# Attention and two MoE layers in one kernel: a new load order, and a new order of the prologue and the ramp

## The chip, the cores and the metric

The kernel runs on one core of a Trainium2 chip. The metric is the time of one execution on the device, in microseconds (us); lower is better. Five engines work side by side, each on its own queue of instructions in a fixed order, and wait for one another by semaphores: PE (TensorE, matrix products), DVE (VectorE), ACT (ScalarE), POOL (GpSimd) and SP (SyncE, which here only issues transfers). Transfers (DMA) are issued from SP's queue and a few from ACT's.

## What is computed

The reference is an attention with pooled keys, and two gated layers behind it:

```python
kv_pool = kv.reshape(B, H // 4, 4, W // 4, 4, C).mean(axis=(2, 4))
k = v = kv_pool.reshape(B, -1, C) @ w_sr            # 768 keys, C = 128
s = (q @ k.T) / sqrt(C)
a = exp(s - s.max(-1)); a /= a.sum(-1) + 1e-9
x = a @ v                                           # 12288 rows of 128
h = x @ moe_w_in;   x = (h * clip(h + 3, 0, 6) / 6) @ moe_w_out     # d_ff = 2048
h = x @ moe2_w_in;  g = where(h >= 1, h, where(h <= -1, 0, (h + 1)**2 / 4))
out = g @ moe2_w_out
```

The weights of the two layers reach the kernel as 64-bit floats, two 32-bit words for an element.

## The kernel before, in words

The 12288 rows are cut into 24 blocks of 512. A block needs its scores (four tiles of 128 rows by 768 keys, `s_mm`), a softmax (`s_max`, `s_exp`, `s_sum`, `a_hi`, `a_lo`), a transpose of the result by DMA, the product with v (`av`), and then layer 1 and layer 2. A layer's 2048 inner columns are walked in eight steps of two slices of 128, and such a step is one *slot*: layer 2 runs 11 slots (`O2`) behind layer 1, and the scores of the next block run beside both. 192 steps of layer 1 follow each other this way. From slot 16 on the order of a slot's parts is the list `SLOT`; the first slots have lists of their own, `RAMP0` and then `RAMP`, and the last ones `TAIL`. All order is written out by hand in these strings, letter by letter; no scheduler moves anything within an engine.

Numbers are kept as pairs of fp16 tiles, a high and a low part, and a product takes three fp16 matmuls (`m_in`, line 759; `m_out`, line 784). Some steps of `m_out` are listed as *whole* (`F32A` for layer 1, `F32` for layer 2): there the fp32 tile itself goes into one fp32 matmul, and the cast (`cast`, line 860) and the low part (`low`, line 868) are left out. `CAST_P` lists the casts that run on POOL instead of ACT, `A_P` the softmax tiles whose fp16 parts are made on POOL (lines 674 and 687) instead of ACT and DVE (676 and 689), `HALF_T` those whose high and low part are transposed by a DMA each (681 and 694) instead of one together (696), `ALT` a second way to make layer 2's activation.

Ahead of the first slot is the prologue, the string `PROLOGUE`: each word is a step, and after each step `load_next` issues as many further loads as there are free buffers. `LOADS` is the order of the loads: `k5` is tile 5 of kv (12 tiles), `w` the next piece of a weight (16 pieces: the four input pieces of layer 1, its four output pieces, then the same of layer 2), `q0` the rows of block 0. All tiles of kv and of the weights are 512 KB and share 17 buffers (12 of tag `wst`, 3 of `g2`, 2 of `t1`); a kv tile frees its buffer when it is pooled, a weight piece when it is converted. k0, k2 and q0 are issued from ACT's queue, all others from SP's (`kv_load`, `q_load`, `w_load`, lines 358, 572, 209 and 212).

The steps of the prologue that matter here:

- `mN`: the largest absolute value of weight piece N, a reduction on DVE (`w_max`, line 229). Even N below 8 are layer 1's input pieces, odd ones its output pieces; 8 to 15 the same of layer 2. `ia it ib ic` make layer 1's input scale from the four maxima by way of PE, `oa ot ob oc` its output scale; `a2 b2 s2` and `a3 b3 s3` do so for layer 2.
- `jN.0`, `jN.1`, `jN.2`: the three stages of converting piece N: two operations on ACT (lines 300 and 302), two on DVE (314 and 316), a cast and a low part on POOL (337 and 340).
- `kN`: pooling of kv tile N on PE. `KV_MODE` has a letter for each tile: P pools with the pooling matrix as the weight (line 387) and needs a copy on ACT and a transpose for each pair of tiles; D takes the tile as the weight (line 392); G adds on POOL first, and a `gN` step does two matmuls (line 407).
- `tM pM zM yM`: keys and values of a group of 128 keys, `q0` and `q1` the transposed and split rows of a block, `vm vr vs vh vl` the scale and the two parts of v.
- `sJ SJ nJ NJ eJ aJ bJ`: block 0's softmax for its tile J: scores of the first and of the second half of the keys, their maxima on DVE, the exponential on ACT, the reciprocal and the high part, the low part with its transpose.
- `x0`, `x1`: the product with v for the two halves of the block, with its high part on ACT and its low part on DVE. After them the first slot begins with `m_in`.
- `d`: an idle matmul on PE whose result is not used.

`MX` hangs prologue steps on slots: in the kernel before it holds seven of layer 2's eight maxima (slots 0 to 3) besides the scales. `CONV_AT` lists the slots in which the remaining nine pieces begin their conversion, `EARLY` the slots of the scores and products of blocks 1 and 2, `SPLIT_AT` those whose scores are done in two halves in the banks of `h` instead of the one score bank.

The loop that plays a slot's list:

```python
def slot(T):
    for n, g in orders[(T >= R0_T) + (T >= RAMP_T) + (T >= TAIL_T)]:
        at, f = ops[n]
        for t in range(served.get(n, 0), T - g + 1):
            key = at(t)
            if key is not None:
                f(*key)
        served[n] = max(served.get(n, 0), T - g + 1)
```

## Time and profile before

| | us |
|---|---|
| median of 3 runs | 1265.27 (1265.13 to 1265.32) |
| the profiled execution | 1266.3 |
| its span, first to last instruction | 1264.5 |
| PE busy in the span | 1230.8 |
| DVE, ACT, POOL busy | 1121.5, 1100.2, 1042.0 |

The span is the part of an execution that the trace covers; 1.8 us of the execution lie around it. A matmul's end is modelled, so a busy PE is not PE at its peak. In the rows further down, "idle before <- releaser" is the time an engine stood still before an instruction, and whose result it had waited for.

### The profile page before, as it was taken

The page shows a single profiled execution, that of the slowest core. Times are in us where ns is not written, and L with a number is a line of the kernel's source. Part 1 is how long each engine was busy: PE and PEld are TensorE (multiplying, and loading weights), DVE is VectorE, ACT ScalarE, POOL GpSimd, SP SyncE. Part 2 cuts the span into 40 slices and gives each one's busy share as a digit, 9 for nine tenths or more (in the row PEclk, how much of TensorE's full clock was granted, in tenths as well). Part 3 has the DMA queues.
Part 4 walks back from the last instruction along what each step waited for, and adds up shares of the span by engine and source line. Part 5 has one row for each costly group of instructions (what it writes and reads, how often), then busy time and mean ns, then how long its engine had stood idle before and what let it go on. Part 6 is the DMA issues. An engine that isn't in the chain of part 4 may idle for free.

```text
span 1264.5 us, 18732 instructions
## 1 busy us (share of the span) xinstructions
PE 1230.8 (97%) x6259; PEld 654.7 (52%) x6259; DVE 1121.5 (89%) x1861; ACT 1100.2 (87%) x1918; POOL 1042.0 (82%) x959
## 2 busy tenths in 40 slices
...
DMA packets 260945, 66.30 MB, mean 52 GB/s; under 512 B 252528, under 2 KB 256752, under 8 KB 260848
## 3 DMA queue, kind: packets, MB, share of 16 engines
...
## 4 chain that ended last, share of the span: by engine, by line
PE 92%; DVE 4%; DMA 2%; ACT 1%; issue 0%; SPq 0%; DVEq 0%; ACTq 0%
PE acc L784 39%; PE h L759 37%; PE s L613 7%; PE s L708 7%; DMA wst<-in_kv_dram 1%; PE s L759 1%; DMA wst<-in_moe_w_out_dram 1%; PE h L387 1%; PE h L708 0%; DVE t L818 0%; DVE g L833 0%; DMA wsr<-in_w_sr_dram 0%; DVE g L849 0%; DVE wst L316 0%; DVE acc L314 0%
## 5 line engine op out<-in xcount | busy, mean ns | idle before, releaser
L868 POOL TENSOR_TENSOR l<-g,h 128x512 f16<-128x512 f32 x351 | 402.8, 1166 | 84.7 <-DVE a L689 57.9
L868 POOL TENSOR_TENSOR l<-t,h 128x512 f16<-128x512 f32 x365 | 431.2, 1202 | 6.5 <-ACT h L860 6.3
L833 DVE TENSOR_SCALAR g<-h,bs 128x512 f32<-128x512 f32 x360 | 274.0, 800 | 31.7 <-PE h L759 31.5
L811 ACT ACTIVATE t<-h,h_sc 128x512 f32<-128x512 f32 x384 | 254.1, 676 | 30.6 <-PE h L759 25.6
L849 DVE SCALAR_TENSOR_TENSOR g<-g,bs,h 128x512 f32<-128x512 f32 x374 | 263.8, 741 | 15.8 <-ACT g L844 13.1
L844 ACT ACTIVATE g<-g,bs 128x512 f32<-128x512 f32 x360 | 243.7, 716 | 18.0 <-DVE g L833 17.4
L818 DVE SCALAR_TENSOR_TENSOR t<-t,h 128x512 f32<-128x512 f32 x384 | 252.8, 679 | 6.0 <-ACT t L811 2.2
L860 ACT CAST h<-g 128x512 f16<-128x512 f32 x346 | 198.3, 614 | 46.9 <-PE acc L784 46.0
L860 ACT CAST h<-t 128x512 f16<-128x512 f32 x361 | 208.2, 616 | 4.9 <-DVE t L818 3.9
L759 PE MATMUL h<-xh,wi0h 128*128 128x512 f16 x384 | 146.4, 381 | 1.4 <-DVE t L818 1.0
L759 PE MATMUL h<-xl,wi0h 128*128 128x512 f16 x384 | 145.5, 379 | 0.1
L759 PE MATMUL h<-xh,wi0l 128*128 128x512 f16 x384 | 145.5, 379 | 0.0
L759 PE MATMUL h<-x2l,wi1h 128*128 128x512 f16 x374 | 141.7, 379 | 0.9 <-POOL x2l L545 0.9
L759 PE MATMUL h<-x2h,wi1l 128*128 128x512 f16 x374 | 141.7, 379 | 0.0
L759 PE MATMUL h<-x2h,wi1h 128*128 128x512 f16 x374 | 141.7, 379 | 0.0
L784 PE MATMUL acc<-l,wo0h 128*128 128x512 f16 x365 | 138.3, 379 | 0.7 <-POOL l L868 0.7
L784 PE MATMUL acc<-h,wo0h 128*128 128x512 f16 x365 | 138.3, 379 | 0.4 <-DVE bs L519 0.4
L784 PE MATMUL acc<-h,wo0l 128*128 128x512 f16 x365 | 138.3, 379 | 0.0
L784 PE MATMUL acc<-h,wo1h 128*128 128x512 f16 x354 | 134.2, 379 | 0.0
L784 PE MATMUL acc<-h,wo1l 128*128 128x512 f16 x354 | 134.2, 379 | 0.0
L784 PE MATMUL acc<-l,wo1h 128*128 128x512 f16 x354 | 134.2, 379 | 0.0
L759 PEld LDWEIGHTS <-wi1h 128*128 128x128 f16 x768 | 75.0, 98 | 94.0 <-issue 5.5
...
## 6 DMA issues: line engine op xcount, KB each, us to landing
out_dram<-o SPq DMA_DIRECT2D x94, 64.0 KB, 1.9
q<-in_q_dram SPq DMA_DIRECT2D x92, 64.0 KB, 2.3
wst<-in_kv_dram SPq DMA_DIRECT2D x7, 512.0 KB, 8.9
wst<-in_moe_w_out_dram SPq DMA_DIRECT2D x7, 512.0 KB, 6.2
wst<-in_moe_w_in_dram SPq DMA_DIRECT2D x6, 512.0 KB, 9.7
...
t<-in_kv_dram SPq DMA_DIRECT2D x3, 512.0 KB, 8.3
g<-in_moe_w_in_dram SPq DMA_DIRECT2D x2, 512.0 KB, 5.2
```

The lines of the kernel that those rows point to most:

```text
L387: nc.tensor.matmul(ps[p0:p0 + 32, :128], pool_m, t[:, g, j], start=(j == 0), stop=(j == 3))
L613: nc.tensor.matmul(ps[h], l[:, js], r[:, ks], start=(n == 0), stop=(n == 2))
L708: nc.tensor.matmul(ps, l[:, k, :], r[:, k, :], start=(n == 0), stop=(n == 3 * KC - 1))
L759: nc.tensor.matmul(ps, l[:, ws], r, start=(n == 0), stop=(n == 2))
L784: nc.tensor.matmul(acc[m], l[:, ws], r[:, k, :], start=(c == 0 and i == 0), stop=(c == NPAIR - 1 and i == len(order) - 1))
L811: nc.scalar.activation(out=g_t[0, s][:, k], in_=h_t[0, s, k], func=ACTF.Relu, scale=h_sc, bias=0.5 * H_SC)
L818: nc.vector.scalar_tensor_tensor(out=g, in0=g, scalar=H_SC, in1=h_t.pop((0, s, k)), op0=ALU.min, op1=ALU.mult)
L833: nc.vector.tensor_scalar(out=g_t[1, s][:, k], in0=h_t[1, s, k], scalar1=bs_t[s // NPAIR][:, 6:7], scalar2=bs_t[s // NPAIR][:, 7:8], op0=A ...
L844: nc.scalar.activation(out=g, in_=g, func=ACTF.Square, scale=bs_t[s // NPAIR][:, 8:9], bias=0.5)
L849: nc.vector.scalar_tensor_tensor(out=g, in0=g, scalar=bs_t[s // NPAIR][:, 6:7], in1=h_t.pop((1, s, k)), op0=ALU.mult, op1=ALU.max)
L860: (nc.gpsimd.tensor_copy if pool else nc.scalar.copy)(out=hl_t[m, s][0][:, k], in_=g_t[m, s][:, k])
L868: eng.tensor_tensor(out=lo[:, k], in0=g_t[m, s][:, k], in1=hi[:, k], op=ALU.subtract)
```

## The change

Only the tables of the order change; no function does. The loads begin with layer 1's weights. All eight maxima of layer 2 become steps of the prologue, in the later part of block 0's softmax and around `x0` and `x1`, and only the scales stay in `MX`. The conversions of pieces 1, 3 and 5 of layer 1 begin earlier in the prologue, and `j2.2` moves into it. Kv tiles 2 and 3 instead of 0 are pooled by mode D, and no tile by mode G. `RAMP0` serves two slots instead of four, and `RAMP0` and `RAMP` have a new order. The lists that choose engines and forms in the first slots change in some entries: `F32A` goes from 19 entries to 16 (slots 0 to 3 lose one each), `F32` from 30 to 32, `ALT` from 20 to 19, `A_P` from 7 to 9, `SPLIT_AT` from 1 to 4.

```diff
-LOADS = "k0 w w k5 k1 k6 w k4 w k3 k2 w k7 q0 k11 k8 w k10 k9 w w w w w w q2 q1 w w w w"
-KV_MODE = "DGPPPPPPPPPP"
+LOADS = "w w k0 w w w k3 w k2 k1 k5 k4 w w k7 k6 k8 k9 q0 k10 k11 w w w w q2 w q1 w w w"
+KV_MODE = "PPDDPPPPPPPP"
 PROLOGUE = """
-m0 k5 m2 g5 k4 k6 k3 m6 m4 ia it ib k1 k2 ic j4.0 t1 j2.0 g4 t2 k0 p1 j4.1 g3 g1 g9 j0.0 g2 k7 j2.1
-j4.2 t3 p3 y1 z1 t0 p0 g8 q0 m3 z0 p2 z3 k8 k11 g10 z2 j0.1 j6.0 j6.1 j6.2 g6 m1 m5 y0 m7 k10 k9 t5
-s0 t4 p5 p4 z5 s1 z4 oa S0 n1 j0.2 s2 y4 S2 n0 S1 N0 n2 N2 N1 d ot y3 e0 y2 e2 e1 a0 y5 s3 vm S3 a1
-a2 d g0 b0 n3 vr b1 vs vh d d d N3 d ob d d e3 b2 g7 q1 d oc a3 vl j5.0 b3 d hs g11 j3.0 j5.1 j3.1 d
-m9 j1.0 x0 Y x1 j1.1 j5.2 j1.2 d j3.2
+m2 m6 m0 m4 ia it m1 ib k3 k0 ic j0.0 j0.1 j2.0 k1 m3 j2.1 t0 j2.2 m5 j4.0 k2 j4.1 m7 t1 k4 oa j0.2
+p0 p1 z0 k5 z1 t2 y0 ot ob j6.0 oc j6.1 j1.0 k7 k6 t3 j4.2 k8 p3 j3.0 k9 y1 p2 k10 j1.1 q0 z2 j3.1 t4
+k11 s0 z3 t5 p4 y2 y3 p5 z4 y4 z5 S0 s2 s1 n0 n1 j5.0 S1 N0 S2 d j5.1 N1 e0 e1 s3 a0 n2 n3 y5 d N2 vm
+m12 vr d e2 b0 S3 a2 a1 N3 d vs e3 b2 q1 a3 vh b1 vl m14 j6.2 b3 m8 m15 d d hs m9 x0 m11 j1.2 m13 Y
+x1 m10 j5.2 d d d j3.2
 """
...
-R0_T = 4
+R0_T = 2
...
-a0 A0 C0:1 G:2 A1 y:1 e:1 o:2 a1 x T:3 f L1:1 B1:2 C1:1 D:1 K0 s Y K1 L0:1 v r0 Q0 O:2 t:1 R:1 r1 H:2
-Q1 l1:1 m0 u:1 c0 U:3 P:1 l0:1 z X0 i:1 F:1 B0:1 j:1 m1 B2:3 X1 n c1 w:1 q
+F:2 G:2 a0 o:2 u:2 A0 H:2 B1:2 a1 O:2 z:1 Y e:1 y:1 x T:4 X1:1 L0:1 r0 C0:1 D:1 K0 t:1 i:1 C1:1 q f
+U:4 A1 m0 v R:1 s w:2 l1:1 L1:1 r1 m1 j:1 B2:4 Q0 K1 B0:1 P:1 c0 X0 c1 l0 n Q1
...
-A_P = ((0, 2), (1, 0), (1, 1), (1, 2), (1, 3), (2, 1), (2, 3))
-HALF_T = ((0, 0), (0, 3), (1, 0), (1, 1), (1, 3))
+A_P = ((0, 0), (0, 2), (1, 0), (1, 1), (1, 2), (2, 0), (2, 2), (2, 3), (3, 0))
+HALF_T = ((0, 1), (0, 2), (0, 3), (1, 1), (1, 3))
...
-F32A = ((0, 0), (0, 1), (1, 0), (1, 1), (2, 0), (2, 1), (3, 0), (3, 1), (4, 0), (5, 0), (5, 1), (6, 0), (7, 0), (8, 1), (9, 0), (10, 0), (10, 1), (11, 0), (12, 1))
+F32A = ((0, 1), (1, 1), (2, 1), (3, 1), (4, 0), (5, 0), (6, 0), (7, 0), (7, 1), (9, 0), (9, 1), (10, 0), (10, 1), (11, 0), (11, 1), (12, 0))
...
-MX = ((0, 'j2.2 m8'), (1, 'm12 m15 m13'), (2, 'm10'), (3, 'm14 a2 m11'), (4, 'b2'), (5, 's2 a3 b3'), (6, 's3'), (7, 'bk'))
+MX = ((2, 'a2 b2'), (3, 'a3 s2'), (4, 'b3'), (5, 's3'), (7, 'bk'))
...
-CONV_AT = (2, 4, 5, 7, 8, 9, 10, 11, 12)
-EARLY = (0, 1, 2, 3, 5, 6, 4, 5, 8, 9, 10, 13, 0)
+CONV_AT = (2, 3, 4, 7, 8, 9, 10, 11, 12)
+EARLY = (0, 1, 2, 3, 5, 6, 4, 5, 8, 10, 9, 13, 0)
...
-SPLIT_AT = (6,)
+SPLIT_AT = (0, 6, 7, 9)
```

## Rows read from the trace of the kernel before

**Rows 1.** The page's first part: busy us, share of the span, instructions.

```profile
PE 1230.8 (97%) x6259; PEld 654.7 (52%) x6259; DVE 1121.5 (89%) x1861; ACT 1100.2 (87%) x1918; POOL 1042.0 (82%) x959
```

**Rows 2.** Timeline of PE, first `m_in`: start, duration, line, out<-in, [idle before <-releaser].

```profile
53.92 0.38 PE L759 MATMUL h<-xh,wi0h 128*128 128x512 f16 x1 [0.35 <-ACT xh L716]
```

**Rows 3.** Sum of the stretches from 53.92 to 120 us: length, busy us by engine.

```profile
sum 66.08, PE 60.52 PEld 33.98 DVE 60.20 ACT 48.43 POOL 50.66; mean PE 4.66 PEld 2.61 DVE 4.63 ACT 3.73 POOL 3.90
```

**Rows 4.** Stretches of ten us: busy us (instructions), PE clock, DMA share, GB/s.

```profile
20.00:30.00 10.00, 8.54 (x98) 7.35 (x96) 7.09 (x23) 6.54 (x18) 3.24 (x3) 1.00 1.08 377
30.00:40.00 10.00, 7.32 (x82) 5.93 (x74) 9.80 (x27) 5.53 (x17) 4.20 (x5) 1.00 0.84 274
```

**Rows 5.** Waits of PE from 53.9 to 120 us: total, times, longest.

```profile
PE acc L784 <- DVE su L662: 1.5, 1, 1.5
PE h L759 <- DVE t L818: 1.0, 2, 0.8
...
PE s L613 <- ACT e L653: 0.8, 1, 0.8
PE acc L784 <- POOL l L868: 0.7, 1, 0.7
```

**Rows 6.** Timeline of DVE: maxima of weights, first conversion step, softmax maxima, low part.

```profile
17.12 1.28 DVE L229 TENSOR_REDUCE mw<-wst 128x1 f32<-128x512 f32 x2 [9.11 <-DMA wst<-in_moe_w_in_dram]
...
23.69 0.69 DVE L314 SCALAR_TENSOR_TENSOR wa<-wa,wr 128x512 uint32<-128x512 uint32 x1 [0.71 <-ACT wr L302]
...
33.17 1.27 DVE L229 TENSOR_REDUCE mw<-wst 128x1 f32<-128x512 f32 x2
...
36.93 0.16 DVE L622 TENSOR_TENSOR nm<-n 128x1 f32<-128x1 f32 x1
...
48.21 1.03 DVE L689 SCALAR_TENSOR_TENSOR a<-e,rc,a 128x768 f16<-128x768 f32 x1
...
60.55 1.28 DVE L229 TENSOR_REDUCE mw<-wst 128x1 f32<-128x512 f32 x2 [1.00 <-DMA wst<-in_moe_w_out_dram]
```

**Rows 7.** DMA issues by line: size, us from issue to landing (k9; q0's first piece).

```profile
t<-in_kv_dram SPq DMA_DIRECT2D x1, 512.0 KB, 8.8
...
q<-in_q_dram ACTq DMA_DIRECT2D x1, 64.0 KB, 7.8
```

**Rows 8.** Timeline of ACT: its first instruction, a copy, a conversion's two operations, an exponential.

```profile
18.01 1.28 ACT L397 ACT_TABLE_LOAD   x1 [18.01 <-DMA q<-in_q_dram]
19.30 0.27 ACT L397 COPY e<-h 128x128 f32<-128x128 f32 x1
...
22.33 0.77 ACT L300 ACTIVATE wa<-wst,ws 128x512 f32<-128x512 f32 x1
22.99 0.67 ACT L302 ACTIVATE wr<-wst 128x512 int32<-128x512 uint8 x1
...
37.13 0.58 ACT L647 ACTIVATE e<-h,nm 128x384 f32<-128x384 f32 x1 [3.22 <-DVE nm L622]
```

**Rows 9.** Timeline of SP's queue: the issue of k9.

```profile
21.55 0.37 SPq L358 DMA_DIRECT2D t<-in_kv_dram  x1
```

**Rows 10.** Timeline of POOL: low part of a softmax tile, of a slot's step, a cast.

```profile
44.19 1.64 POOL L687 TENSOR_TENSOR a<-e,a 128x768 f16<-128x768 f32 x1
...
79.61 1.15 POOL L868 TENSOR_TENSOR l<-t,h 128x512 f16<-128x512 f32 x1
...
94.00 0.61 POOL L860 CAST h<-t 128x512 f16<-128x512 f32 x1 [2.00 <-DVE t L818]
```

**Rows 11.** Chain that ended last: start, us, four fp32 and six fp16 products.

```profile
65.99 1.72 PE acc L784 x4
67.71 1.29 PE h L759 x6
```

**Rows 12.** Waits of SP's queue up to 80 us: total, times, longest.

```profile
SPq L209 <- DMA g<-in_kv_dram: 3.0, 1, 3.0
```

**Rows 13.** Stretches of two us, columns as in rows 4.

```profile
40.00:42.00 2.00, 1.52 (x5) 1.33 (x6) 1.60 (x7) 2.00 (x5) 0.00 (x0) 0.54 0.82 119
```

More of the change, by code (lines that the diff above doesn't have):

```diff
@@ L35 @@
 W_DT = (FP16, FP16)
-R0_T = 4
+R0_T = 2
 RAMP_T = 16
 RAMP0 = """
-G:1 a0 H:4 a1 i:1 v:1 Y:1 c0 l1:2 Q1:1 F:2 e:1 s x A0:2 f X1 r0 K1:1 Q0:1 B2:3 B0:1 c1 K0:1 C1:3 R:3
-m1:1 t:1 D:2 j:3 L0:3 U:4 n B1:2 q m0 u:2 A1 P:3 y:1 l0 w:2 L1:2 o:1 X0 z T:4 C0 r1 O:2
+Q0 x Q1:1 F:3 U:3 a0 o:2 f:1 C1:2 z:1 K1:1 s l1:1 r0 B1:3 K0:2 a1 L1:3 G:2 R:2 A1 T:4 m0 B0:2 X0:2
+q:1 e:1 r1 Y:1 w:2 D:1 t:1 c0 C0 y v n P:1 j:2 B2:1 X1:2 l0 i:1 O:2 u:1 m1 L0:3 H:4 A0:2 c1
 """
 RAMP = """
-a0 A0 C0:1 G:2 A1 y:1 e:1 o:2 a1 x T:3 f L1:1 B1:2 C1:1 D:1 K0 s Y K1 L0:1 v r0 Q0 O:2 t:1 R:1 r1 H:2
-Q1 l1:1 m0 u:1 c0 U:3 P:1 l0:1 z X0 i:1 F:1 B0:1 j:1 m1 B2:3 X1 n c1 w:1 q
+F:2 G:2 a0 o:2 u:2 A0 H:2 B1:2 a1 O:2 z:1 Y e:1 y:1 x T:4 X1:1 L0:1 r0 C0:1 D:1 K0 t:1 i:1 C1:1 q f
+U:4 A1 m0 v R:1 s w:2 l1:1 L1:1 r1 m1 j:1 B2:4 Q0 K1 B0:1 P:1 c0 X0 c1 l0 n Q1
 """
@@ L58 @@
-HALF_T = ((0, 0), (0, 3), (1, 0), (1, 1), (1, 3))
+CAST_P = ((0, 0, 0), (0, 0, 1), (0, 1, 0), (0, 2, 0), (0, 2, 1), (0, 3, 0), (0, 3, 1), (0, 4, 0), (0, 4, 1), (0, 5, 1), (0, 6, 1), (0, 7, 1), (0, 8, 1), (0, 9, 0), (0, 9, 1), (0, 12, 0), (1, -12, 1), (1, -10, 0), (1, -10, 1), (1, -9, 1), (1, -8, 0), (1, -8, 1), (1, -7, 0), (1, -6, 0), (1, -6, 1), (1, -4, 0), (1, -3, 0), (1, -3, 1), (1, -2, 0), (1, -2, 1), (1, -1, 1), (1, 2, 0), (1, 3, 0), (1, 4, 0), (1, 4, 1))
+A_P = ((0, 0), (0, 2), (1, 0), (1, 1), (1, 2), (2, 0), (2, 2), (2, 3), (3, 0))
@@ L59 @@
+HALF_T = ((0, 1), (0, 2), (0, 3), (1, 1), (1, 3))
 IDLE_W = 2
-ALT = ((-12, 1), (-11, 1), (-10, 1), (-8, 0), (-7, 0), (-7, 1), (-6, 0), (-5, 1), (-4, 0), (-4, 1), (-2, 0), (-1, 0), (1, 1), (3, 1), (9, 0), (10, 1), (12, 0), (16, 1), (17, 0), (17, 1))
-ALT_P = ((3, 1), (8, 1), (17, 0))
-F32A = ((0, 0), (0, 1), (1, 0), (1, 1), (2, 0), (2, 1), (3, 0), (3, 1), (4, 0), (5, 0), (5, 1), (6, 0), (7, 0), (8, 1), (9, 0), (10, 0), (10, 1), (11, 0), (12, 1))
-F32 = ((-11, 0), (-11, 1), (-10, 0), (-9, 0), (-8, 0), (-8, 1), (-7, 1), (-6, 1), (-5, 0), (-5, 1), (-4, 0), (-3, 1), (-2, 0), (-2, 1), (-1, 0), (-1, 1), (0, 0), (0, 1), (1, 0), (1, 1), (2, 1), (3, 0), (3, 1), (4, 0), (4, 1), (8, 1), (10, 1), (11, 0), (13, 0), (16, 0))
```

4 lines of the change are left out of this document (3 added, 1 removed).

## The prediction

> **What bounds the kernel now.** The page's head comes first: PE is busy 97% of the span and no other engine reaches 90% [rows 1]. What can be gained lies in PE's idle time, 1264.5 - 1230.8 = 33.7 us. The table by stretches, read next, puts it at the start. PE's first matmul of block 0's first pair starts at 53.92 us [rows 2]; everything before it is the prologue. From there to 120 us PE is busy 60.52 of 66.08 us, so 5.6 us are idle [rows 3]. From 120 us on the lists of the order are the same in both kernels.
>
> What holds the prologue? Between 20 and 40 us the transfers run at 377 and then 274 GB/s, and DVE goes from 7.09 to 9.80 busy us of ten [rows 4]: first the loads, then DVE. What holds PE after 53.92 us stands in the list of its waits: 1.5 us for DVE's `su`, 1.0 for DVE's `t`, 0.8 for an exponential on ACT, 0.7 for POOL's `l` [rows 5]. The first is told by DVE's own timeline: at 60.55 us it stood 1.00 us before two maxima of layer 2, because their weight piece had not landed, and `su` is queued behind them [rows 6]. So a maximum in the wrong place costs PE time.
>
> **The change, part by part.**
>
> *Loads.* Layer 1's four input pieces become tiles 1, 2, 4 and 5 of the list; now they are 2, 3, 7 and 9, and DVE's last two maxima for them start at 17.12 us after 9.11 us of idling [rows 6]. With 512 KB a tile and 377 GB/s a place in the list is 0.524 / 0.377 = 1.4 us [rows 4, 7], so the piece in place 5 instead of 9 comes some 5.6 us earlier, near 11.5 us. The scale from these maxima then no longer holds up the first conversion; ACT does. ACT begins at 18.01 us, when its last issue for q0 is out [rows 8]. One table load (1.28) and one conversion's ACT part (0.77 + 0.67 = 1.44) later, at 20.7 us, DVE can take its first conversion step, which ran at 23.69 [rows 6, 8]: DVE's queue moves 3 us earlier. This wait is new on DVE: m3 and everything behind stands behind it, which is harmless as long as ACT does start at 18.
>
> The price is paid by kv. Its last tile goes from place 18 to 20. k9, the last now, was issued at 21.55 us and took 8.8 us, so it landed at 30.35 [rows 7, 9]. Two places are +2.8 us at most, 33.1; at least it is 30.5, since k9's own issue was held while the queue had others to move. I take the middle, 31.7.
>
> *From the last kv tile to the first exponential.* Now that is 37.13 - 30.35 = 6.8 us [rows 8]. The end of the maximum before it is DVE's at 36.93 + 0.16; between stand work that does not belong to the chain, as the two maxima of 1.27 us at 33.17 [rows 6] and the two conversions ahead of them. In the changed order these steps (m5, m7, j6.1, j1.1) stand well ahead of k11, and DVE, three microseconds earlier, has room for them. I cut the 6.8 by 2.3 (those two maxima, 1.3, and one and a half of the four conversion steps at 0.69, 1.0) to 4.5: first exponential at 36.2, **0.9 us earlier**. Bounds: 30.5 + 4.5 = 35.0 (-2.1), and 33.1 + 6.8 = 39.9 (+2.8).
>
> *Block 0's softmax.* From the end of that maximum to the end of the last low part of `a` (48.21 + 1.03 = 49.24) DVE needs 12.15 us now [rows 6]. Added in this stretch: j5.1 (0.69 + 0.69), m12 and m14 (0.64 each), 2.7 us. Gone from it: the low part of j=0 to POOL (1.03), three maxima of v and the scale of layer 1's output piece, nine short ones at 0.16 or so, 1.4. Net **+0.2 us**. POOL takes that low part at 1.64 us [rows 10]; it is idle there, and the pair's other half, j=1, is on DVE and later, so it hides; if POOL were late, the first half's transpose would be, by at most 1.64 - 1.03 = 0.6. SP issues seven transposes instead of six there and no weight loads behind them; its queue has no work between.
>
> *m8, m15, m9, m11, m13.* They run between that low part and the first pair, 53.92 - 49.24 = 4.7 us in which DVE now does two conversions, one maximum and the scales. Five times 0.64 is 3.2, no more than the conversions' 2.8 and one maximum: hidden, but m11 and m13 stand between x's two low parts, so I book **+0.2**. Bounds: 0 and 1.3 (both in full). All pieces must have landed by then. The last four are issued behind q1 instead of behind the transposes; at 377 GB/s 15.5 MB (28 tiles and three q) take 41 us plus the start, so near 45 us.
>
> First pair: -0.9 + 0.2 + 0.2 = **-0.5 us**, bounds -1.9 and +4.3.
>
> *The ramp.* Six maxima (0.64) and j1.1 (1.38) leave DVE after the first pair, 5.2 us; three more split scores of block 1 put back about 1.1 (one more short minimum, one more sum and a second reduction's start each). The 1.5 us before `su` go with their cause; the 0.8 before the score tile goes too, since split scores use the h banks and DVE reaches the maximum sooner. Of the rest, 3.3 us, DVE's `t` waits halve (-0.5). POOL gets worse: the whole pairs (one fp32 product, no cast and no low part) go from 19 to 16 in layer 1, each 0.61 + 1.15 us on POOL or partly on ACT [rows 10], and four of them are now missing in the first four slots; +0.4 for PE's wait on it. **-2.4 us**; bounds 0 (new waits replace the old) and -5.6 (all idle time goes).
>
> *PE's own work.* Four fp32 products take 1.72 us, six fp16 ones 1.29 [rows 11]: a whole pair is 0.43, three fp16 products 0.65. Layer 1 loses three whole pairs, layer 2 gains two: +0.22 us. Three idle matmuls fewer and one tile more by mode D instead of G (12 matmuls more at 8.54 / 98 = 0.09, 1.0 us [rows 4]) lie where PE waits anyway; were the 1.46 us of idling there gone, D would cost its 1.0. The moved casts between ACT and POOL, ALT, HALF_T and the one-slot moves of CONV_AT and EARLY I put at 0: PE is ahead of them by a slot; without that cover a late one costs what `l` does now, 0.7.
>
> Sum: -0.5 - 2.4 + 0.2 = **-2.7 us**. The profiled execution took 1266.3 us (span 1264.5), 1.0 above the median 1265.27; it would become 1263.6, the median **1262.6**.
>
> **The rivals.** *Slower: ACT starts late.* DMA issues wait for earlier ones to land: a weight piece in SP's queue waited 3.0 us for k0, of which it needs nothing [rows 12], and ACT sat until 18.01 us behind q0's issues [rows 8]. q0 goes from place 14 to place 19 of the list. If its four issues are held by the tiles that stand eight ahead of it in the new list, the last waits for k8, seven tiles of 1.4 us later than now: ACT starts at 18.0 + 9.8 = 27.8. Before the first exponential ACT has six conversions (8.6) and about 18 copies of 0.27 plus q0's, some 14 us, and the maximum's 0.7 between, so it comes at 42.5 instead of 37.13: +5.4 +0.2 for PE -2.4 for the ramp = +3.2, **1268.5**. It decides from the point where ACT's first compute is later than 22.5 us (22.5 + 14 + 0.7 = 37.2). For it speaks the wait that the rows show; against it, that nothing in ACT's queue stands between k2 and q0, so the issues may be held by early tiles as now: 0.22. The Trainium skill (DMA: Bandwidth & Descriptors, Queues, rings and completion order) says that each DMA engine takes turns between the queues that have work; by that q0, once issued, does not stand behind SP's longer list. The trace agrees as far as it goes: q0's first piece landed after 7.8 us while SP's queue was full [rows 7]. By it, landing adds nothing to this rival's price.
>
> *No change.* DVE, 98% busy from 30 to 40 us, has no room: the maxima and j5.1 push the first pair by their 2.7 + 1.3 less the 1.4 and 1.0 that left, +1.6, kv adds the 1.4 of one place, PE its 0.2, and the ramp gives its 2.4: +0.8, **1266.1**. 0.26.
>
> *The clock.* PE's granted clock was 0.54 of full between 40 and 42 us, the 1.2 GHz level for most of it, after ten microseconds in which PE was busy 7.32 [rows 4, 13]. Nine idle matmuls instead of twelve could let the first pairs run at that level: a pair's six products of 1.29 us would take twice that, and two pairs with their scores some 2.6 us more: 1262.6 + 2.6 = **1265.2**. 0.05. The Trainium skill (TensorE: Matmul & The Clock Gate, What's actually happening) has the low clock as the resting state that activity lifts, a rule that speaks against removing idle matmuls; the row agrees.
>
> **How the numbers follow.** A measurement of this kernel tells some 0.2% (2.5 us) from no change. Faster by more: 0.47, the forecast. Within: 0.31 (the second and third rivals). Slower: 0.22. Low end: -1.9 - 5.6 + 0.2 = -7.3, nearly all, 1258.2. High end: the slower rival, 1268.5, with a little beyond left out.
>
> **What would show it.** Right: first conversion on DVE near 21 us; first exponential near 36; first pair near 53.4; no DMA wait before a maximum after it; PE idle from there to 120 us near 3.2 us instead of 5.6. Wrong: ACT's first compute after 22.5 us, x's low parts held by maxima, or PE waits for POOL's `l` in the first four slots.

## The result: 1.1% slower, and the profile after

The changed kernel takes 1281.05 us (median of 5 runs, 1276.80 to 1281.31) against 1265.32 for the kernel before (5 runs beside it): ratio 1.0113, 95% interval 1.0101 to 1.0126. The forecast was 1262.6 with a range up to 1268.5 and a little beyond. One run of the five took 1276.8; a likely cause of these 4 us comes up with the experiments. The profiled execution took 1280.9 us, its span is 1279.1, 14.6 longer than before. First the page's head, busy us and share of the span [rows 1]: PE is busy 9.0 us more, and idle 14.6 - 9.0 = 5.6 us more.

```profile
PE 1239.8 (97%) x6269; PEld 660.9 (52%) x6269; DVE 1124.4 (88%) x1862; ACT 1099.5 (86%) x1917; POOL 1045.7 (82%) x965
```

The timeline of PE (start, us, engine, line, operation, tiles, count, [idle before <- what ended it]) shows the place. The first pair starts at 70.46 us, 16.5 later than before [rows 2]. From there to the end it takes 1279.1 - 70.46 = 1208.6 us, against 1264.5 - 53.92 = 1210.6: the ramp gained 2.0. All of the loss, and more, is in the prologue.

```profile
12.81 0.37 PE L243 MATMUL h<-ident,mw 128*1 128x128 f32 x1 [12.81 <-DVE mw L238]
14.12 3.63 PE L392 MATMUL h<-pool_m,wst 128*128 128x32 f32 x16
21.10 3.46 PE L392 MATMUL h<-pool_m,wst 128*128 128x32 f32 x16
24.49 1.92 PE L387 MATMUL h<-wst,pool_m 128*32 128x128 f32 x16
...
33.78 1.07 PE L387 MATMUL h<-wst,pool_m 128*32 128x128 f32 x16
38.31 1.07 PE L387 MATMUL h<-g,pool_m 128*32 128x128 f32 x16
...
60.92 0.37 PE L708 MATMUL h<-at,vh 128*128 128x256 f16 x1 [9.71 <-DMA at<-a]
64.79 1.65 PE L708 MATMUL h<-at,vh 128*128 128x256 f16 x7 [1.16 <-DMA at<-a]
70.46 0.38 PE L759 MATMUL h<-xh,wi0h 128*128 128x512 f16 x1
```

L392 is a kv tile pooled by mode D, L387 one by mode P. The two D tiles take 3.63 and 3.46 us, and a P tile 1.92 at 24 us and 1.07 at 34: PE works at half pace until about 28 us, with hardly a gap: it is busy 13.63 of the 14 us from 14 us on. The last line but one begins 24 products (six of the first, 18 of the second) that end at 69.89, at 0.21 us each.

The stretches tell the rest (columns as in [rows 4]; the last but one of each line is the DMA share, ahead of it stands the clock). Between 30 and 40 us the DMA share is 0.47, it was 0.84; from 50 to 60 PE has 1.21 us of work; from 50 to 70 the granted clock is 0.50 and 0.52, which is the 1.2 GHz level (it falls to it between 49.0 and 49.5 us). In the 66.08 us after the first pair PE is busy 61.98, 60.52 before [rows 3].

```profile
20.00:30.00 10.00, 9.27 (x64) 7.67 (x61) 3.55 (x6) 2.70 (x8) 5.06 (x6) 1.00 0.91 287
30.00:40.00 10.00, 8.67 (x114) 6.78 (x115) 7.15 (x17) 6.20 (x16) 1.27 (x1) 1.00 0.47 159
50.00:60.00 10.00, 1.21 (x3) 0.15 (x1) 9.25 (x21) 4.99 (x8) 8.27 (x8) 0.50 1.10 279
60.00:70.00 10.00, 7.92 (x38) 5.34 (x39) 3.25 (x11) 0.54 (x2) 2.23 (x3) 0.52 0.59 109
70.46:136.54 66.08, 61.98 (x292) 34.94 (x291) 59.50 (x127) 52.06 (x89) 49.26 (x52) 1.00 0.30 57
```

Why the DMA engines run dry stands in SP's queue. L358 issues k9 at 21.93 us, but k10 and k11 only at 28.31 and 28.79: the group of three spans 7.26 us. The next weight piece is out only at 36.52, the last three from 49.97, and the seven transposes follow behind them, the first with 4.35 us in the queue. Below the queue's timeline stand its two longest waits between 20 and 60 us (what waits <- for what: total, times, longest).

```profile
21.93 7.26 SPq L358 DMA_DIRECT2D g<-in_kv_dram  x3
36.52 1.98 SPq L209 DMA_DIRECT2D g<-in_moe_w_in_dram  x2
...
49.97 2.15 SPq L212 DMA_DIRECT2D wst<-in_moe_w_out_dram  x3
52.22 4.35 SPq L696 DMA_TRANSPOSE at<-a  x1
56.67 2.54 SPq L681 DMA_TRANSPOSE at<-a  x2
59.31 1.24 SPq L694 DMA_TRANSPOSE at<-a  x1
60.64 1.24 SPq L681 DMA_TRANSPOSE at<-a  x1
61.97 2.57 SPq L694 DMA_TRANSPOSE at<-a  x2
```

```profile
SPq L209 <- PE h L387: 7.2, 1, 7.2
SPq L358 <- DMA q<-in_q_dram: 5.9, 1, 5.9
```

One reason is in `stage`: each tag hands out its buffers in rotation, so a tag whose oldest tile is alive gives none, though younger ones are dead. Seventeen tiles fill all buffers. k9, k10 and k11 are tiles 18 to 20 and go to the three `g2` buffers of two weight pieces and k0, and the pieces after them to those of k9 and k10: hence the wait of 7.2 us until PE has pooled k9. The wait of 5.9 us ahead of k10 is another. Its buffer was dead at 23.44 us, when POOL had made the low part of the piece in it; the trace has the issue wait until q0's first issue had landed at 28.22, of whose data k10 needs nothing, and that issue had stood in ACT's queue until 24.60.

Last ACT's timeline. Its table load and first conversion come early (18.01 and 19.30 us before [rows 8]); q0's four issues now stand in mid-queue, and ACT idles 2.72 us there; the first exponential is at 43.55, 37.13 before.

```profile
5.37 1.28 ACT L300 ACT_TABLE_LOAD   x1 [5.37 <-DMA g<-in_moe_w_in_dram]
15.00 0.76 ACT L300 ACTIVATE wa<-g,ws 128x512 f32<-128x512 f32 x1 [8.34 <-DVE ws L276]
...
24.60 2.94 ACTq L572 DMA_DIRECT2D q<-in_q_dram  x4
27.59 0.28 ACT L427 ACTIVATE kTh<-h 128x128 fp32r<-128x128 f32 x1 [2.72 <-DMA q<-in_q_dram]
...
43.55 0.58 ACT L647 ACTIVATE e<-h,nm 128x384 f32<-128x384 f32 x1 [0.99 <-DVE nm L622]
```

### The profile page after: what moved, and what is told of

It is laid out like the page before. It is cut to its first block, busy times and chain, and to the rows that moved or that the text cites. A ratio compares the mean times of both kernels' runs of the same rounds, so it can differ in the third digit from the quotient of the medians.

```text
span 1279.1 us, 18764 instructions
## 1 busy us (share of the span) xinstructions
PE 1239.8 (97%) x6269; PEld 660.9 (52%) x6269; DVE 1124.4 (88%) x1862; ACT 1099.5 (86%) x1917; POOL 1045.7 (82%) x965
## 4 chain that ended last, share of the span: by engine, by line
PE 93%; DVE 2%; POOL 1%; ACT 1%; DMA 1%; SPq 0%; issue 0%; DVEq 0%; ACTq 0%; POOLq 0%
PE acc L784 39%; PE h L759 37%; PE s L613 7%; PE s L708 7%; PE h L387 1%; PE h L708 1%; DMA t<-in_moe_w_in_dram 1%; PE h L392 1%; PE s L759 1%; DVE g L849 0%; POOL a L687 0%; DMA at<-a 0%; PE h L421 0%; DVE mw L229 0%; DVE t L818 0%
## 5 line engine op out<-in xcount | busy, mean ns | idle before, releaser
L811 ACT ACTIVATE t<-h,h_sc 128x512 f32<-128x512 f32 x384 | 254.1, 675 | 31.0 <-PE h L759 26.9
```

The source lines that it names most:

```text
L811: nc.scalar.activation(out=g_t[0, s][:, k], in_=h_t[0, s, k], func=ACTF.Relu, scale=h_sc, bias=0.5 * H_SC)
```

## The experiments

Seventeen kernels. The table gives for each the median, the ratio to the kernel before with its interval, and from its profiled execution the first exponential, the first pair, the time between them, and the time from the first pair to the end (us). Code for loads and steps is the changed kernel's unless said otherwise.

| kernel | median | ratio | first exp. | first pair | between | rest |
|---|---|---|---|---|---|---|
| before | 1265.3 | | 37.13 | 53.92 | 16.8 | 1210.6 |
| after | 1281.05 | 1.0113 (1.0101 to 1.0126) | 43.55 | 70.46 | 26.9 | 1208.6 |
| prologue_only | 1277.63 | 1.0099 (1.0085 to 1.0113) | 43.71 | 70.48 | 26.8 | 1209.4 |
| ramp_only | 1266.83 | 1.0013 (1.0003 to 1.0023) | 37.08 | 53.57 | 16.5 | 1211.1 |
| fill | 1275.33 | 1.0088 (1.0070 to 1.0106) | 39.98 | 64.13 | 24.2 | 1208.8 |
| warm | 1280.87 | 1.0113 (1.0099 to 1.0126) | 43.81 | 70.96 | 27.2 | 1208.6 |
| warm_long | 1278.31 | 1.0102 (1.0087 to 1.0117) | 40.34 | 65.98 | 25.6 | 1208.6 |
| gate | 1274.48 | 1.0073 (1.0058 to 1.0088) | 40.06 | 62.71 | 22.7 | 1209.1 |
| rotate | 1275.58 | 1.0083 (1.0066 to 1.0100) | 41.93 | 64.40 | 22.5 | 1208.7 |
| soft | 1277.50 | 1.0097 (1.0082 to 1.0112) | 40.30 | 67.34 | 27.0 | 1208.8 |
| gate_fill | 1275.23 | 1.0076 (1.0063 to 1.0089) | 40.06 | 61.69 | 21.6 | 1209.1 |
| gate_fill_b0 | 1277.82 | 1.0098 (1.0084 to 1.0112) | 39.78 | 64.45 | 24.7 | 1208.9 |
| mend | 1275.22 | 1.0081 (1.0066 to 1.0095) | 40.59 | 62.16 | 21.6 | 1208.6 |
| before_a0_pool | 1268.81 | 1.0034 (1.0021 to 1.0047) | 36.40 | 57.47 | 21.1 | 1210.0 |
| mend_order | 1272.58 | 1.0050 (1.0036 to 1.0064) | 41.22 | 59.79 | 18.6 | 1211.0 |
| mend_order_ot | 1273.00 | 1.0063 (1.0045 to 1.0080) | 41.55 | 60.05 | 18.5 | 1210.5 |
| before_fill | 1266.15 | 0.9992 (0.9980 to 1.0004) | 36.58 | 53.19 | 16.6 | 1210.2 |
| all_p | 1274.98 | 1.0064 (1.0042 to 1.0086) | 38.49 | 64.51 | 26.0 | 1208.7 |
| mend_scale | 1273.85 | 1.0052 (1.0035 to 1.0069) | 38.89 | 57.45 | 18.6 | 1212.1 |

**Which half?** Two kernels cross the tables.

prologue_only:

```diff
 # after's LOADS, KV_MODE, PROLOGUE, MX, block 0 of A_P and HALF_T
-R0_T = 2
+R0_T = 4
 # also as before: RAMP0, RAMP, CAST_P, ALT, ALT_P, F32A, F32,
 # CONV_AT, EARLY, SPLIT_AT, blocks 1 and 2 of A_P and HALF_T
```

> The changed kernel with its ramp's tables put back (orders of the ramp, whole pairs, casts, CONV_AT, EARLY, SPLIT_AT, blocks 1 and 2 of A_P and HALF_T as before); the loads, the prologue, block 0 and MX stay changed. Theory 1: the loss sits ahead of the first pair, which starts near 70.5 us as in the changed kernel (53.92 before): 1265.3 + 16.5 = 1281.8, less at most 2 us for the maxima that have left the ramp: 1280 to 1282. Rival: the new ramp depends on the prologue and each half costs by itself; then the first pair still comes near 70.5 but the time lies outside 1278 to 1284.

The first pair came at 70.48 us; the profiled execution took 1281.64, the median is 1277.6. Theory 1 holds for the place.

ramp_only:

```diff
 # before's LOADS, KV_MODE, PROLOGUE, MX, CONV_AT, block 0 of A_P and HALF_T
-R0_T = 4
+R0_T = 2
 # also as after: RAMP0, RAMP, CAST_P, ALT, ALT_P, F32A, F32,
 # EARLY, SPLIT_AT, blocks 1 and 2 of A_P and HALF_T
```

> The kernel before with the changed ramp's tables (R0_T, RAMP0, RAMP, CAST_P, ALT, ALT_P, F32A, F32, EARLY, SPLIT_AT, blocks 1 and 2 of A_P and HALF_T); the loads, the prologue, block 0, MX and CONV_AT stay as before. The first pair stays near 53.9 us in every theory. Theory 1, as predicted: the ramp's gain comes from the maxima that leave DVE; here they stay, so nothing is gained and PE's own work and POOL cost 0.2 + 0.4: 1265.9, within 1.0 of the kernel before. Rival: the gain of 2.0 us after the first pair (1210.6 to 1208.6 in the profiles) sits in the tables: 1263.3.

1266.83 beside 1266.03 for the kernel before: +0.8, where theory 1 had +0.6. The new tables alone gain nothing; the ramp's 2.0 us need the maxima to be gone.

**PE's pace.** Two kernels fill PE's waits with idle matmuls.

```diff
-... hs m9 x0 m11
+... hs m9 d d d d (45 times) x0 m11
```

> The changed kernel with 45 more idle matmuls ahead of block 0's first product with v, in the 9.7 us in which PE waits there for a transpose. They compute nothing that is used. In the changed kernel the granted clock is 0.50 from 50 to 68 us and the second product takes 5.12 us, against 2.14 before. Theory 1: the low clock is a part of the loss by itself; the granted clock stays near 1.00 there, each product takes near 2.2 us, the first pair comes 3 to 5 us earlier and the time is 1276 to 1278. Rival: the transposes set the end and the low clock only fills waits: the products get shorter but the first pair moves by less than 1 us, 1280 to 1282.

The stretch from first exponential to first pair fell from 26.9 to 24.2 us with the granted clock at 0.97 from 50 to 70 us: the low clock costs by itself, theory 1. But the first pair came 6.3 us earlier, beyond theory 1's 3 to 5, and 3.6 of that lie ahead of the edit: the profiled execution had its first exponential at 39.98 instead of 43.55. PE's timeline of that run shows why:

```profile
14.13 3.63 PE L392 MATMUL h<-pool_m,wst 128*128 128x32 f32 x16
...
21.01 1.87 PE L392 MATMUL h<-pool_m,wst 128*128 128x32 f32 x16
22.81 1.07 PE L387 MATMUL h<-wst,pool_m 128*32 128x128 f32 x16
```

The second D tile ran at full pace. Up to here the two programs are the same, so PE's pace rises near 21 us in some executions and near 28 in others, and the first exponential moves by 3.6 us with it. Those are probably the two times, 1277 and 1281: the traces with the late rise are of executions of 1280.9, 1281.4 and 1281.6 us (after, warm, prologue_only), this one's is of 1274.65. There is only one trace of each kernel, so it is not shown.

The step between is PE's last product for kv, k11's (38.31 + 1.07 = 39.38 in the changed kernel):

```profile
34.74 1.07 PE L387 MATMUL h<-g,pool_m 128*32 128x128 f32 x16
```

Here it ends at 35.81, and the first exponential starts 4.17 us behind that end in both. k11 landed at 33.26 and 33.27. In 14 of the 15 profiles with the new prologue the distance from this end to the first exponential is 4.16 to 4.18 us, for exponentials from 38.49 to 43.81; in the kernel before it was 5.27 (31.86 to 37.13). So PE's end sets the first exponential, and between these two runs that end does not follow k11's landing.

```diff
+W W W W (16 times)
 m2 m6 m0 m4 ia it m1 ib k3 k0 ic ...
+def warm_mm():
+    nc.tensor.matmul(mem["warm"][:, :128], ident, ident)
```

> The changed kernel with 16 idle matmuls of the identity ahead of PE's first instruction (12.81 us). They compute nothing that is used. In the changed kernel the two tiles of mode D take 3.63 and 3.46 us, where the one before took 1.87, and tiles of mode P 1.85 to 1.92 until about 28 us, then 1.07. Theory 1: PE's early pace holds the prologue; the tiles take about 1.9 and 1.1 us from the start, PE gains some 5 us before 28 us, the first exponential (43.55) comes 2 to 4 us earlier and the time is 1277 to 1279. Rival: the last tiles' arrival holds it (k11 lands near 33.7 us): the first exponential moves by less than 1 us, 1280 to 1282.

Nothing moved: the 16 ended at 7.15 us, and PE idled 5.4 us behind them. But this trace records the clock from the start. The tile at 20.87 us took 3.46 us as in the changed kernel, and the clock stands at 0.50 beside it (lines of this run are one higher):

```profile
20.87 3.46 PE L393 MATMUL h<-pool_m,wst 128*128 128x32 f32 x16
```

```profile
22.00:24.00 2.00, 2.00 (x11) 2.00 (x11) 1.34 (x2) 0.59 (x2) 1.15 (x1) 0.50 1.05 407
```

So the half pace is the 1.2 GHz level, with PE busy but for one gap of 0.36 us from 14 to 28 us.

```diff
-W W W W (16 times)
+W W W W (40 times)
```

> The changed kernel with 40 idle matmuls of the identity ahead of PE's first instruction. The 16 of the earlier run ended at 7.15 us, PE then idled 5.4 us, and the granted clock was 0.50 from 14 to 28 us; the run that filled the later wait happened to have its second tile of mode D at 1.87 us instead of 3.46 and its first exponential at 39.98 instead of 43.55 us. 40 of them, at 0.22 each, last until about 12.4 us. Theory 1: PE's pace holds the prologue; the clock stays at the upper level from 12.8 us on, both tiles of mode D take 1.87, the first exponential comes at 38.5 to 40 us, and the time is 1275 to 1277.5 in every round. Rival: PE's pace is set by what it runs (mode D's short matmuls) and not by what ran before: the first tile takes 3.6 us again and the time is 1277 or 1281 as before.

Both D tiles ran at full pace (1.97 and 1.87 us). The first exponential came at 40.34, just past theory 1's 38.5 to 40 and no earlier than in the runs whose pace rose at 21 us, and two of the four times, 1279.3 and 1279.5, lie above its bound. Theory 1 holds for the pace of the D tiles alone. Two things in the trace may have taken its place, and were not separated: the clock fell to 0.59 and 0.56 from 20 to 24 us, and ACT idled 5.86 us behind q0's issues.

```profile
20.09 6.07 ACTq L573 DMA_DIRECT2D q<-in_q_dram  x4
26.20 0.28 ACT L428 ACTIVATE kTh<-h 128x128 fp32r<-128x128 f32 x1 [5.86 <-DMA wst<-in_kv_dram]
```

**SP's queue.** Three kernels on the same stretch.

```diff
-LOADS = "... q2 w q1 w w w"
+LOADS = "... q2 w q1 b w w w"
+            if k == "b":
+                if ("w", (0, 3)) not in did:
+                    return
-MX = ((2, 'a2 b2'), (3, 'a3 s2'), ...
+MX = ((2, 'a2 b2 m11'), (3, 'm13 m15 a3 s2'), ...
```

> The changed kernel with its last three weight pieces issued behind block 0's transposes instead of ahead of them, and the maxima m11, m13 and m15 that need them in MX at slots 2 and 3, as the kernel before has such ones. Theory 1: the late pieces on SP's queue (issued 49.97 to 52.12 us) hold the transposes, of which the first took 4.35 us to issue and 7.0 to land; the first transpose is out by 51.7 us, the first product with v starts 3 to 5 us earlier (60.92 now), the first pair 1.5 to 4 us (70.46 now). Rival: DVE's last low part, which ends at 58.82, sets the end and not SP: the first pair moves by less than 1 us.

The stretch fell from 26.9 to 22.7 us, theory 1; against the runs with the early rise whose stretch is otherwise unchanged (25.6 in warm_long, 26.0 in all_p, 27.0 in soft) the gain is 3.0 to 4.4. The first transpose took 1.61 us in the queue instead of 4.35:

```profile
46.77 1.61 SPq L696 DMA_TRANSPOSE at<-a  x1
49.08 2.55 SPq L681 DMA_TRANSPOSE at<-a  x2
```

```diff
-LOADS = "w w k0 w w w k3 w k2 k1 k5 ...
+LOADS = "w w k0 w w k3 k2 w w k1 k5 ...
```

> The changed kernel with tiles k3 and k2 two and three places earlier in the list of loads, so that they lie at the head of the rotation of the large staging pool, and not the piece for layer 1's output, which dies late. k9 is then issued behind k3's pooling instead of behind a conversion (21.93 us), k11 behind the first conversion, and the next weight pieces no longer behind k9's pooling (36.52). Theory 1: the held loads cost time ahead of the first pair: k11 lands near 30 us (33.7), the weight pieces are out some 10 us earlier, the transposes find SP's queue empty, and the first pair comes 3 to 6 us earlier: 1275 to 1278 beside 1281, or 1271 to 1274 where PE's clock rises early. Rival: PE and DVE hold it and the loads were hidden: less than 1 us.

22.5 us from exponential to pair: the same 4.4 us from the other side, since the last pieces were out by 42 us. k11 landed at 32.01, not near 30 as theory 1 had it. The first exponential, at 41.93, came later than in the other runs with the early rise, because m1's piece, which DVE takes ahead of the first scale, was now later and PE's first tile started at 16.07; the times, 1274.6 to 1276.4, lie above theory 1's 1271 to 1274 for such runs.

```diff
-... e3 b2 q1 a3 vh b1 vl m14 j6.2 b3 m8 ...
+... e3 b2 a3 b1 b3 q1 vh vl m12 m14 j6.2 m8 ...
```

> The changed kernel with the last two low parts of block 0's softmax ahead of q1's transpose, v's split and the maxima m12 and m14 on DVE. In the changed kernel these stand between the low parts, the last of which ends at 58.82 us, 15.3 us behind the first exponential (12.1 before). Theory 1: what was put into the softmax costs: the last low part ends some 3 us earlier and the first pair 2 to 3 us. Rival: the transposes on SP's queue, seven of 1.25 us behind weight pieces, hold the first pair anyway: less than 1 us.

The low parts ended at 52.8 us, 12.5 behind the first exponential, and the stretch did not move (27.0 us). Theory 1 falls: while SP's queue holds the transposes, these 2.8 us on DVE are free.

**Together.**

```diff
 # as gate, and
-hs m9 x0 j1.2
+hs m9 d d d d (20 times) x0 d d d d d j1.2
```

> The run with the last three weight pieces behind the transposes, and 20 idle matmuls ahead of block 0's first product with v and 5 ahead of the second, sized to PE's waits there (4.92 and 1.34 us). They compute nothing that is used. From the first exponential to the first pair it took 26.9 us in the changed kernel, 24.15 with the fill alone, 22.65 with the late pieces moved alone, 16.8 in the kernel before. Theory 1: the two losses are separate and add up: 19 to 20.5 us here, time 1271 to 1273 where PE's early pace rises at 21 us, 4 us more where it rises at 28. Rival: with the transposes earlier PE's wait is too short for the clock to fall, so the fill gives less than 1 us: 22 us or more.

21.6 us: 1.0 less than gate alone, where adding up asked for 2.2 to 3.7 and the rival for less than 1; the result lies between the two. At 58 to 60 us the granted clock is 0.50 in gate and 1.00 here. The 24 products behind the last wait took 4.7 us in gate and 2.6 here, but the five matmuls behind x0 turned out to stand in front of work (1.07 us), as the first product's last six terms wait for the same transpose.

```diff
-A_P = ((0, 0), (0, 2), ...        HALF_T = ((0, 1), (0, 2), (0, 3), ...
+A_P = ((0, 2), ...                HALF_T = ((0, 0), (0, 3), ...
```

> The same as the run with pieces behind the transposes and fill, and block 0's entries of A_P and HALF_T as in the kernel before: the high and low part of j=0 on ACT and DVE instead of POOL, six transposes instead of seven. Theory 1: the seventh transpose (1.25 us of SP's queue) and POOL's two-part chain are what is left of the loss between first exponential and first pair: that stretch falls by another 1 to 3 us against the run without this edit. Rival: DVE, which gets 1.03 us back and shares the stretch with five more maxima, holds it: no change or up to 1 us longer.

3.1 us longer: theory 1 falls, and the rival was too mild. The edit moves j=0 off POOL and also changes which transposes are single, and the clock was at 0.50 again from 58 to 60 us; which of these costs the 3 us was not separated.

```diff
 # as rotate, warm_long and the fills of gate_fill, and
-ia it m1 ib k3 k0 ic j0.0 j0.1 j2.0 k1
+ia it ib k3 k0 ic j0.0 j0.1 j2.0 m1 k1
```

> The changed kernel with k3 and k2 earlier in the list of loads, m1 behind the first scale on DVE so that PE's first tile does not wait for it, 40 idle matmuls at the start and 20 + 5 ahead of the products with v: the causes named so far mended together, layer 2's maxima and the softmax as the change has them. Theory 1: first exponential near 38 to 39 us, 19.7 us from there to the first pair, so the first pair at 57.5 to 59 us and the time 1268 to 1270, in all rounds alike. Rival: what the softmax now holds on DVE and POOL takes the place of what is mended: first pair after 61 us, 1272 or more.

The rival's place: first pair at 62.16 us, with a time of 1275.2. 8.3 of the 16.5 us are mended; six transposes stood back to back on SP from 49.6 to 57.5 us.

```diff
 # kernel before
-A_P = ((0, 2), (1, 0), ...
+A_P = ((0, 0), (0, 2), (1, 0), ...
```

> The kernel before with one part of the change alone: block 0's j=0 of the softmax on POOL (the entry (0, 0) added to A_P). It takes 1.0 us of low part off DVE, which is busy without a gap from 43.9 to 53.4 us, and gives POOL 0.82 + 1.64 us, idle from 37 to 43 us; the transposes of j=0 come later, by at most 1.5 us. Theory 1: DVE's queue holds the first pair in the kernel before, so the last low part (48.21) comes up to 1 us earlier and the time is 1264.2 to 1265.1. Rival: POOL's chain of j=0 pushes that of j=2 behind it by 1.5 us, whose transpose feeds the second product: the first pair comes later by 0.5 to 1.5 us, 1265.7 to 1266.7.

+3.8 us, and 4.3 from exponential to pair: the rival's side, over twice its upper bound of 1.5, and by another route, j=0's own transposes instead of j=2's. j=0's low part reaches SP at 44.71 us (42.68 before). The first product starts at 49.91, 47.86 before, behind a wait of 4.21 us, and after that wait the clock is at 0.50:

```profile
49.91 0.59 PE L708 MATMUL h<-at,vh 128*128 128x256 f16 x2 [4.21 <-DMA at<-a]
```

```profile
50.00:52.00 2.00, 2.00 (x10) 1.39 (x10) 1.97 (x4) 1.34 (x2) 0.00 (x0) 0.50 1.08 206
```

In the kernel before the idle matmuls leave a wait of 0.59 us at that place. So 2 us of the loss are the later transposes, and the rest fits the products at the low clock; no run fills this wait to show it.

**The softmax's order and the first exponential.**

```diff
 # as mend; A_P, HALF_T of block 0 as before, and behind k11:
-S0 s2 s1 n0 n1 j5.0 S1 N0 S2 d j5.1 N1 e0 e1 s3 a0 n2 n3 y5 d N2 ...
+S0 s1 n0 s2 N0 S2 S1 n2 N2 n1 N1 d e0 e2 e1 a0 y5 s3 vm S3 a1 a2 ...
-... b3 m8 m15 d d hs m9 x0 m11
+... b3 d d d hs j5.1 m12 m14 d d d d d x0 d d d d d j6.2 m8 m15 m9 Y x1 m11
```

> The run with loads, maxima m1 and both fills mended, and behind k11 the steps of block 0's softmax in the order of the kernel before, with its entries of A_P and HALF_T (six transposes; j=0 not on POOL), the maxima m8, m9, m12, m14, m15 behind the last low part or behind the first product with v. In the mended run the first exponential came at 40.59 and the first pair at 62.16 us: 21.6 us, of which 12.7 behind the last exponential (8.3 in the kernel before), where seven transposes stood back to back on SP from 49.6 to 57.5 us. Theory 1: the order of the softmax is what is left: from first exponential to first pair 17 to 19 us, the first pair at 57.5 to 59.5 us, time 1268 to 1270. Rival: it is DVE's load and the maxima wherever they stand: 20.5 us or more, 1271 or more.

18.6 us, theory 1's stretch, and the pair at 59.79, just outside its bounds. The time is not what it said, 1272.6 instead of 1268 to 1270, and PE's timeline tells why (lines one higher):

```profile
59.79 0.38 PE L760 MATMUL h<-xh,wi0h 128*128 128x512 f16 x1 [0.35 <-ACT xh L717]
62.09 0.59 PE L760 MATMUL h<-xl,wi0h 128*128 128x512 f16 x1 [1.93 <-DVE xl L723]
```

The pair's second product waits 1.93 us for x1's low part, which stands on DVE behind three maxima and a wait of 0.66 us for the piece of two of them. Behind that wait the clock is low (0.57 from 62 to 66 us; 1.00 in mend). In mend the second product came at 62.68. So the order of the softmax gives 3.0 us up to the first pair, and the time behind it grows by 2.4, from 1208.6 to 1211.0: the profiled spans of the two are both 1270.8, and their medians, 1275.2 and 1272.6, differ by 2.6 without a cause that these traces show. The edit moved the maxima, the softmax's steps and the entries of A_P and HALF_T together.

```diff
 # as mend_order, and
-y0 ot ob j6.0 oc j6.1 j1.0 k7 k6 t3 j4.2 k8 p3
+y0 j6.0 k7 k6 t3 j6.1 j4.2 k8 ot ob oc j1.0 p3
```

> The same, and the scale of layer 1's output piece (ot, ob, oc) behind k8's pooling on PE instead of ahead of k7's. In the mended run PE waits there for DVE's maximum of late pieces until 26.24 us (0.79 and 0.51 us), k7 and k6 are pooled only at 27.32, at 2.59 us instead of 1.54, and from 30.27 us on PE runs without a gap to k11's end at 36.4, 4.2 us ahead of the first exponential. Theory 1: that wait in PE's queue holds the first exponential: it comes 1.5 to 2.5 us earlier than in the run beside it. Rival: the last tiles' landing or ACT's copies hold it: less than 0.7 us.

No gain (41.55), though theory 1's step was right for PE: with a low early pace (3.44 us for the first D tile, 1.97 beside it) its last kv product still ended 1.2 us earlier, at 35.83 instead of 37.04. The way from there took 5.72 us, the one exception to the 4.17: PE now waited four times, 0.23 to 0.50 us, for results of DVE and POOL, with DVE's conversions between. So PE's queue was not the only bound; mend_scale takes it up.

```diff
 # kernel before
-N1 d ot y3 e0 ...      x0 Y x1
+N1 d d d d d d d ot y3 e0 ...      x0 d d d d d Y x1
```

> The kernel before with six more idle matmuls where PE waits 1.80 us ahead of the last scores of block 0 (40.48 us; the granted clock is 0.54 and 0.60 from 40 to 44 us there), and five ahead of the second product with v (1.23 us). They compute nothing that is used. Theory 1: the low clock at these scores lies on the way to the first pair: the scores (2.5 us) take 1.0 us less, the first pair comes 0.3 to 0.9 us earlier, time 1264.1 to 1264.8. Rival: DVE, busy without a gap from 43.9 to 53.4 us, sets that pace and the scores have slack: within 0.2 us of the kernel before.

The clock stayed at 1.00 from 40 to 44 us, and the time within 0.1% of before: the rival, DVE sets that pace. The low clock ahead of these scores costs nothing in the old order; ahead of the products with v it cost 2.7 us in the new one (fill).

```diff
-KV_MODE = "PPDDPPPPPPPP"
+KV_MODE = "PPPPPPPPPPPP"
```

> The changed kernel with k2 and k3 pooled by mode P like the other ten tiles, instead of mode D: one part of the change undone. Theory 1: mode D costs at PE's lower pace, where its two tiles take 3.63 and 3.46 us against 1.85 to 1.92 for a tile of mode P; PE is the bound there, so the first exponential (43.55 us) comes 1.5 to 3.5 us earlier, and no round shows the 4 us between 1277 and 1281, since PE's long stretch at the lower pace is shorter: 1275 to 1279. Rival: mode P adds a copy on ACT and a transpose on PE for k2 and k3 (0.27 and 0.33 us and a wait between them), and what follows is held by other queues: first exponential within 0.7 us of 39.98 or 43.55, whichever state the round is in.

Theory 1's direction, with more than it asked (5.1 us instead of 1.5 to 3.5): the first exponential at 38.49, PE's last kv product ending at 34.32 instead of 39.38, and five runs between 1273.1 and 1275.7. Against an execution with the early rise (fill, 39.98) the step is worth 1.5, and its median gain, 6.1 us, is no larger than gate's 6.6.

```diff
 # as mend_order; w9, w10, q2, q1 ahead of the other late pieces in LOADS, and
-y0 ot ob j6.0 oc j6.1 j1.0 k7 k6 t3 j4.2 k8 p3 j3.0 k9 y1 p2 k10 j1.1 q0 z2 j3.1 t4
+y0 j6.0 k7 k6 t3 j6.1 j4.2 k8 p3 k9 y1 p2 k10 q0 z2 t4
-... N1 d e0 ...  N3 d d d e3 ...  q1 d a3 ...  hs j5.1 m12 m14 ...
+... N1 d ot e0 ...  N3 d ob d d e3 ...  q1 d oc a3 ...  hs j1.0 j5.1 j3.0 j1.1 j3.1 ...
+MX = ((1, 'm12 m14'), (2, 'a2 b2 m9 m11'), (3, 'm13 m15 a3 s2'), ...
```

> The run with loads, fills and block 0's softmax mended, and the scale of layer 1's output piece (ot, ob, oc) and the conversions that hang on it (j1, j3) behind the first exponential, as in the kernel before; layer 2's maxima but m8 and m10 then stand in MX at slots 1 to 3, since their pieces come later. Theory 1: this scale and these conversions, put ahead of the last kv tiles in PE's, ACT's and DVE's queues, hold the first exponential: it comes at 38 to 39.5 us (41.22 in the run beside it, 37.13 in the kernel before), the first pair at 56.5 to 58, and the ramp takes the maxima, 1211 us from the first pair on: 1269 to 1271. Rival: the last kv tiles, of which k11 is place 20 of the list, land too late for that: first exponential after 40 us.

38.89 and 57.45 us, both in theory 1's bounds, though PE's early pace was low here too (3.46 and 1.98 us). The rest grew to 1212.1: the pair's second product waits 1.75 us for x1's low part, now behind conversions. The seven runs lie at 1270.2 to 1271.4 and 1273.9 to 1274.3.

No kernel tried beats the one before. Most of the steps that brought the first pair nearer to 53.92 us put a piece of that kernel back, and with the last ones the gain behind it was gone.

## Why the prediction was wrong

**The step that failed is the first pair**, -0.5 us in the sum, +16.5 in the trace: +6.4 ahead of the first exponential, +10.1 behind it.

*Loads: the early part was right and worth nothing.* DVE's first conversion came at 16.34 us (20.7 forecast, 23.69 before). ACT did not wait for q0's issues at its start: its table load ran at 5.37 us and its first conversion at 15.00, where the prediction had it begin at 18.

*k11: just above the upper bound.* The prediction priced places in the list. k10 and k11 were held by q0's landing, and k11 landed at 33.26 us, where 31.7 was forecast and 33.1 was the bound.

*From the last kv tile to the first exponential: 4.5 us forecast, 10.3 measured* (33.26 to 43.55). The prediction let this way begin at the landing. It begins where PE gets to the tile: k11's product starts 5 us behind its landing. From the product's end on the way did get shorter, 4.17 us instead of 5.27, much as forecast. The 6.4 us are PE's end, 39.38 instead of 31.86, +7.5, less these 1.1.

*Mode D: "lie where PE waits anyway".* This is the sentence that cost most. PE was booked as idle in the prologue; with the first weight pieces and their scale ahead of the first kv tile it starts at 12.81 instead of 9.28 us and then has hardly a gap. The two D tiles at the lower clock take 3.63 and 3.46 us of this path, where the prediction had 1.0 for mode D were it not covered; without them PE's last kv product and the first exponential come 5.1 us earlier (all_p, one profile each). In executions where the pace rises at 21 us the same step is worth some 1.5.

*Block 0's softmax: "its queue has no work between".* SP had the last three weight pieces there, since its queue had been held behind the rotation of the buffers. That is 4.3 us (gate, and 4.4 by rotate). The order of the softmax with its tables is a further 3.0 (mend to mend_order), of which 2.4 came back behind the first pair. DVE's term was forecast at +0.2: from the first exponential to the end of the last low part it was 15.3 us against 12.1, but with the transposes held on SP the 2.8 that soft took off it moved nothing. The low clock in the products is 1.0 net once the pieces are out of the way, 2.7 alone.

The parts behind the first exponential sum to 4.3 + 1.0 + 3.0 = 8.3 of 10.1; 1.8 stay open, as do 1.3 of the 6.4 ahead of it. The latter are PE's end too (34.32 in all_p, 2.5 later than before, less 1.1), but why PE ends late without mode D is not shown: its first tile starts 5.0 us later than before (14.27, 9.28) and k11 lands 2.2 later (32.59, 30.35). The output piece's scale and conversions, ahead of the last kv tiles, are a third candidate (mend_scale, 2.3 us against mend_order), but that run changed several things at once. The parts were measured in different company, so the sum is a bookkeeping and no proof.

*The maxima and the ramp: right.* -2.0 us against -2.4 less PE's own 0.2, that is -2.2. The reason holds too: tables alone +0.8, and with the maxima alone gone the rest is 1209.4 (prologue_only), 1.2 of the 2.0; the other 0.8 come only with both. The maxima between x's low parts cost nothing here, as DVE idles 2.00 us behind them, ahead of the second low part; in mend_order the second product waits 1.93 us there, once the transposes are in time.

*The rivals.* The slower one, ACT behind q0's issues, did not happen at its place, ACT's first compute being at 15.00 us and not past 22.5; its mechanism, issues that wait for earlier ones to land, came up in mid-queue, 2.72 us on ACT here and 5.86 in warm_long, and 5.9 on SP ahead of k10; by the traces of after and fill the last did not set the first exponential. The clock rival had the right mechanism and 0.05: it looked at the first pairs, where the clock was 1.00, and not at the products ahead of them or the pooling. No rival had SP's queue late with the transposes, or PE as the prologue's bound, so the range ended 12.5 us short of the time. For the clock the Trainium skill (TensorE: Matmul & The Clock Gate, What's actually happening) has how busy PE has lately been decide between the two levels; the fall after PE's wait of 4.21 us agrees (before_a0_pool, 0.53 from 49 to 50 us), as does the changed kernel's, at 49.0 to 49.5 us, after PE had been busy 2.82 of the 5 us before; the long stay at 0.50 with PE busy does not by itself.
